# Softmax of the taps on one partition, exchanged weight halves by DMA, and the last product split

## The chip, the cores and the metric

The kernel runs on one core of a Trainium2 chip. A core has TensorE (PE; its weight loads are listed as PEld), VectorE (DVE), ScalarE (ACT), GpSimd (POOL) and SyncE (SP), which work from queues of their own and wait for each other by semaphores, and 16 DMA engines that all queues share. SP and ACT issue DMAs whose descriptors are made by hardware (queue q1 and q10 in the profile); POOL issues DMAs whose descriptors are made by software (q0). The metric is the time on the device of one execution in microseconds (us), less is better.

## The reference

Two stages in a row. First a light convolution along the sequence: x has 8 sequences of 3904 tokens of 192 channels, a softmax over 7 taps is made for each of 8 heads, and each head's 24 channels are summed over the current and the six tokens before with these taps. Then a multiplicative feed-forward over all 31232 tokens.

```python
w = softmax(weight)                       # 8 heads x 7 taps
out = np.einsum('hk,bskhg->bshg', w, x_unf)   # 7 tokens, ending at s
...
a = x @ w1                                # 192 -> 1024
b = x @ w2                                # 192 -> 1024
h = a * b @ w3                            # 1024 -> 1024
return (h @ w_out).astype(np.float32)     # 1024 -> 192
```

## The kernel before

The tokens are cut into two halves of 15616 (r = 0, 1) that are worked on side by side: partitions 0 to 63 belong to the one and 64 to 127 to the other, in x, in the convolution and in the transposed activations.

*Convolution.* x comes in blocks of windows of 64 tokens (58 new ones each; `SIZES`), loaded by POOL and cast to bf16 (`load_x`, and `load_first` for the very first window, lines 89 to 130). The taps are turned into band matrices `Aband`: the softmax (lines 178 to 191, on all 128 partitions, each having its own copy of the 8 x 7 taps by the DMA of line 133) gives `wsb`; `band_taps` (line 203) multiplies it with shifted diagonals into `cprod`; `band_sum` (line 210) adds these up on PE with an identity and with a swapped identity. `conv` multiplies a block's windows with the bands. Block 0 is convolved in lines 427 to 430 before all else; blocks 1 and 2 between rounds of the first two products.

*First product* (`first_product`, line 340). For each chunk R of 512 tokens of each half there are 8 rounds ft, one for each 128 of the 1024 columns. In a round PE makes pa = x w1 and pb = x w2 of both halves, 6 matmuls of 64 rows each, ACT copies pa to bf16, and DVE multiplies the copy by pb into `abT`. The work of `between` is put behind the round that it names: in chunk 0 the convolution of block 1 stands behind rounds 2 and 4 and its transposes behind round 6.

*Why halves are exchanged.* A matmul of half r reads x on partitions 64 r to 64 r + 63, and needs its 64 rows of the weights on the same partitions. `wn` holds the weights as loaded (three tiles), `wsw` the same with the two halves of the partitions exchanged; `w_of` chooses between them. `load_w` loads columns in two parts, 0 to 767 and 768 to 1023. `swap_w(k, part, engines)` copies one part of `wn[k]` to `wsw[k]` in two instructions; the parts are set by `WC`:

```python
WC = (0, DFF // 2, DFF * 3 // 4, DFF)
```

Part 0 of k = 0 and 2 and all of parts 1 and 2 are copied by POOL, part 0 of k = 1 by DVE and ACT.

*Second product* (`second_product`, line 367). w3 and w_out are multiplied together once (`W_sb`), so each chunk's `abT` is multiplied by `W_sb` alone: 8 matmuls for each 128 tokens, into one PSUM tile for a chunk and half. ACT copies the tile to SBUF and SP stores it. The last chunk has 256 tokens, so its last product has 16 matmuls, one copy of 384 columns, and one store.

*Warm-ups.* `warm(n)` gives PE n matmuls on zeros, whose results are not read: 18 at the start (line 172), two ahead of the first product (`lead=2`).

*Order.* The order of the instructions on each engine is that of the program text (`manual_schedule`); the framework adds the waits. POOL's queue holds, in this order: x of block 0, the first window, the masks (identity and diagonals), `load_w` of 768 columns, x of block 1, the four copies of part 0, `load_w` of the last 256 columns, x of block 2, the twelve copies of parts 1 and 2, w_out, w3, x of blocks 3 and 4. SP issues nothing before the stores of convolved rows of block 2. All PSUM tiles take turns in four buffers.

Of the kernel before, what the change touches and what calls it, by code (L numbers as in the profile page):

```python
# [8 lines left out]
FP32 = mybir.dt.float32  # L9
BF16 = mybir.dt.bfloat16  # L10
AX = mybir.AxisListType
ALU = mybir.AluOpType
# [4 lines left out]
def kernel(  # L17
# [10 lines left out]
    nc = tc.nc  # L28

    B, S, D = x.shape  # L30
    H, K = weight.shape
    G = D // H
    DFF = moe_w1.shape[1]
# [3 lines left out]
    NS = 2  # L37
# [28 lines left out]
    def banks(name):  # L66
        return psum.tile([128, NS, CH], FP32, tag="banks", name=name)
# [4 lines left out]
    def slot(shape, dtype, name):  # L72
        return stage.tile(shape, dtype, tag="slot", bufs=5, name=name)
# [15 lines left out]
    def load_x(b, parts=(0, 1)):  # L89
        tiles = xb_of.setdefault(b, [])  # L90
        zeros_of = zero_rows.setdefault(b, [])
        for i0, n in [v for e, v in enumerate(halves_of(b)) if e in parts]:
            xb = work.tile([128, n, D], BF16, tag="xb", bufs=6, name="xb")
            w = 0
            if i0 == 0:
                nc.vector.memset(xb[:, 0, :], 0.0)
                for r in range(NS):
                    nc.gpsimd.dma_start(out=xb[Q * r:Q * r + Q, 1:n, :], in_=x_spans(r, 1, n - 1))
                w = n
            while w < n:  # L100
                i = i0 + w
                m = min(n - w, WB - i % WB)
                at_end = i + m == NWIN
                if at_end:
                    m -= 1
                if m:
                    for r in range(NS):
                        nc.gpsimd.dma_start(out=xb[Q * r:Q * r + Q, w:w + m, :],  # L108
                                            in_=x_spans(r, i, m))
                if i % WB == 0:  # L110
                    zeros_of += [(xb, 0, w), (xb, 1, w)]
                w += m
                if at_end:
                    nc.gpsimd.memset(xb[Q:128, w, :], 0.0)
                    t = tok(NWIN - 1) - PAD
                    nc.gpsimd.dma_start(out=xb[0:Q, w, :], in_=x_rows[t:t + Q, :])
                    nc.gpsimd.dma_start(out=xb[Q:Q + PAD + LAST, w, :],
                                        in_=x_rows[TS + t:TS + t + PAD + LAST, :])
                    w += 1
            if len(halves_of(b)) == 1:  # L120
                tiles += [(xb, 0), (xb, SIZES[b] // 2)]
            else:
                tiles.append((xb, 0))


    def load_first():
        xb = xb_of[0][0][0]
        for r in range(NS):
            nc.gpsimd.dma_start(out=xb[Q * r + PAD:Q * r + Q, 0, :],
                                in_=x_rows[r * TS:r * TS + ST, :])  # L130

    wall = const.tile([128, H, K], FP32)
    nc.scalar.dma_start(out=wall, in_=weight.partition_broadcast(128))
    load_x(0)
    load_first()

    tiny = const.tile([128, 1], FP32)
    nc.vector.memset(tiny, 0.0)
# [2 lines left out]
    nc.scalar.activation(out=tiny, in_=tiny, func=ACT.Exp)  # L141

    ones = const.tile([128, 1], BF16)
    nc.gpsimd.memset(ones, 1.0)
    identw = const.tile([128, 128 + Q], BF16)
    diag = const.tile([128, Q + PAD], BF16)
    for m in (identw[:, 0:128], identw[:, 128:128 + Q], diag[0:Q], diag[Q:128]):
# [19 lines left out]
    def warm(n, t=None):  # L167
        t = banks("warm") if t is None else t
        for j in range(n):
            nc.tensor.matmul(t[:, j % 2, :], zeros[:, 0:128], zeros, start=True, stop=True)  # L170

    warm(18)


    wmax = const.tile([128, H], FP32)
    wsum = const.tile([128, H], FP32)
    wsb = const.tile([128, 2, 2, K], BF16)
    nc.vector.reduce_max(out=wmax, in_=wall, axis=AX.X)
    nc.vector.tensor_tensor(
        out=wall, in0=wall, in1=wmax.unsqueeze(2).to_broadcast([128, H, K]), op=ALU.subtract)  # L180
    nc.scalar.activation(out=wall, in_=wall, func=ACT.Exp)
    nc.vector.reduce_sum(out=wsum, in_=wall, axis=AX.X)
    nc.vector.reciprocal(out=wsum, in_=wsum)
    for r in range(NS):
        ps = slice(Q * r, Q * r + Q)
        nc.vector.tensor_tensor(
            out=wsb[ps],
            in0=wall[ps].rearrange("p (g a e) k -> p g a e k", g=2, a=2)[:, :, r],
            in1=wsum[ps].rearrange("p (g a e) -> p g a e", g=2, a=2)[:, :, r].unsqueeze(3)
                .to_broadcast([Q, 2, 2, K]),  # L190
            op=ALU.mult)

    Aband = const.tile([128, 2, 2, 2, Q], BF16)

# [142 lines left out]
    def width(R):  # L337
        return min(CH, TS - R * CH)

    def first_product(R, between=None, lead=0):  # L340
        N = width(R)
        ab = work.tile([128, JT, NS, CH], BF16, tag="abT", bufs=LAG + 1, name="abT")
        abT_of[R] = ab
        r0 = (R * CH) % RING
        for ft in range(JT):
            pq = []
            for i in range(2):
                p = banks("pa" if i == 0 else "pb")
                pq.append(p)
                if ft == 0 and i == 0:  # L350
                    warm(lead, p)
                for k in range(NP):
                    for r in range(NS):
                        rs = slice(Q * r, Q * r + Q)
                        nc.tensor.matmul(  # L355
                            p[:, r, 0:N], w_of(i, k, r)[rs, ft * 128:(ft + 1) * 128],
                            xT[k][rs, r0:r0 + N],
                            start=(k == 0), stop=(k == NP - 1))
            pa, pb = pq
            asb = work.tile([128, NS, CH], BF16, tag="asb", bufs=3, name="asb")  # L360
            nc.scalar.copy(out=asb[:, :, 0:N], in_=pa[:, :, 0:N])  # L361
            nc.vector.tensor_tensor(out=ab[:, ft, :, 0:N], in0=asb[:, :, 0:N],  # L362
                                    in1=pb[:, :, 0:N], op=ALU.mult)
            if between and ft in between:
                between[ft]()

    def second_product(R, r):
        ab = abT_of[R]
        ng = width(R) // 128
        ops = banks("ops")  # L370
        for g in range(ng):
            for jt in range(JT):
                nc.tensor.matmul(  # L373
                    ops[:, g // 2, (g % 2) * D:(g % 2) * D + D],
                    ab[:, jt, r, g * 128:(g + 1) * 128], W_sb[:, jt, :],
                    start=(jt == 0), stop=(jt == JT - 1))
        osb = slot([128, ng, D], FP32, "osb")
        nc.scalar.copy(out=osb.rearrange("p (a g) d -> p a (g d)", g=2),  # L378
                       in_=ops[:, 0:ng // 2, 0:2 * D])
        t0 = r * TS + R * CH  # L380
        nc.sync.dma_start(
            out=out[t0:t0 + ng * 128, :].rearrange("(g p) d -> p g d", p=128), in_=osb)
        if r == 1:
            del abT_of[R]

# [62 lines left out]
    def seq(*fs):  # L448
# [42 lines left out]
    for p, rounds in enumerate(phases):  # L491
        b, e = PROLOGUE_BLOCKS + p // 2, p % 2
        if b < NB:
            for xb, r, w in zero_rows.pop(b, []):
                nc.gpsimd.memset(xb[Q * r:Q * r + PAD, w, :], 0.0)
        for j, R in enumerate(rounds):
            first_product(R)
            if j == 0 and b + 1 < NB:
                P(out=pace, in_=abT_of[R][0:1, JT - 1, 1, 0:2])  # L499
                load_x(b + 1, (0, 1) if p == 1 else (e,))  # L500
        last = NR if p == len(phases) - 1 else done + 2
        for i in range(done, last):
# [39 lines left out]
```

## Time and profile before

| | us |
|---|---|
| median of 3 runs | 530.91 (530.59 to 531.13) |
| profiled execution, its own time | 530.57 |
| its span, first to last instruction | 528.9 |
| TensorE busy | 521.7 |
| first matmul of the first product | 12.55 |
| last matmul ends | 524.64 |

The profile page gives busy times of engines over the span, the chain of work that ended last (followed back from the last instruction to what released each step), groups of instructions by line, and the DMA queues. A row of a timeline is: start in us, length in us, engine, line, operation, output <- inputs, shapes, count, and in brackets how long the engine had been idle and what ended that. "PEclk" on the page is the clock that the throttle granted; it is at 9 tenths or more in all 40 slices.

### The profile page before, as it was taken

To read this page: it belongs to the slowest core of one execution; us is meant where nothing else is said; L and a number is where in the kernel's file an instruction comes from. 1 tells how busy PE (TensorE), PEld (TensorE's weight loads), DVE (VectorE), ACT (ScalarE), POOL (GpSimd) and SP (SyncE) were. 2 spreads that over 40 slices of the span, in tenths; PEclk is the share of its full clock that TensorE was granted. 3 is DMA by queue.
4 is the path that set the end of the run, shared out by engine and by line. 5 is a ranking of instruction groups with operands and counts; after the bars stand their busy time and mean duration, and the time that the engine had idled before them with its cause. 6 is when DMAs were issued, how large, how long until landed. Compare 5 with 4: busy or idle time off the path is not lost.

```text
span 528.9 us, 12698 instructions
## 1 busy us (share of the span) xinstructions
PE 521.7 (99%) x5469; PEld 351.0 (66%) x5469; DVE 359.3 (68%) x337; ACT 316.2 (60%) x348; POOL 54.8 (10%) x102
## 2 busy tenths in 40 slices
PE   8999999999999999999999999999999999999996
PEld 4555975857658576585765857667585574846676
DVE  4779459397593976949669496794957849386460
ACT  3887557375573755737467374664746647375652
POOL 8841002011010100201001010020000000000000
PEclk9999999999999999999999999999999999999999
DMA  9999559979562894636956379554725055240204
GB/s 117 110 206 191 116 96 189 184 165 143 131 90 95 173 132 131 87 114 138 147 148 70 123 147 135 133 56 134 150 81 120 1 151 127 78 90 23 99 2 151
DMA packets 130541, 63.13 MB, mean 119 GB/s; under 512 B 83352, under 2 KB 129460, under 8 KB 130484
## 3 DMA queue, kind: packets, MB, share of 16 engines
q1 hardware_dynamic: 91764, 45.65, 35.7%
q0 software_dynamic: 38576, 16.63, 27.0%
q8 instruction: 43, 0.70, 0.6%
q14 instruction: 14, 0.11, 0.1%
q10 hardware_dynamic: 144, 0.03, 0.0%
HBM read 33.28 MB, written 34.82 MB: 129 GB/s over the span
## 4 chain that ended last, share of the span: by engine, by line
PE 96%; DVE 2%; ACT 1%; issue 0%; ACTq 0%
PE ops L373 31%; PE pa L355 30%; PE pb L355 29%; PE cps L249 2%; PE warm L170 1%; DVE abT L362 1%; ACT asb L361 1%; PE wps L413 1%; PE tps L302 1%; PE w3ps L404 0%; PE bps L215 0%; ACT convo L266 0%; DVE w3T L407 0%; DVE convo L423 0%; ACT osb L378 0%
## 5 line engine op out<-in xcount | busy, mean ns | idle before, releaser
L362 DVE TENSOR_TENSOR abT<-asb,pb 128x1024 bf16<-128x1024 bf16 (+1 forms) x248 | 298.3, 1204 | 45.8 <-ACT asb L361 29.3
L361 ACT CAST asb<-pa 128x1024 bf16<-128x1024 f32 (+1 forms) x248 | 247.6, 998 | 70.4 <-PE pa L355 69.7
L355 PE MATMUL pb<-xT,wn 64*128 64x512 bf16 (+1 forms) x744 | 201.8, 372 | 0.2
L355 PE MATMUL pa<-xT,wn 64*128 64x512 bf16 (+1 forms) x744 | 197.9, 373 | 0.5
L355 PE MATMUL pa<-xT,ws 64*128 64x512 bf16 (+1 forms) x744 | 198.0, 373 | 0.0
L355 PE MATMUL pb<-xT,ws 64*128 64x512 bf16 (+1 forms) x744 | 193.8, 373 | 0.0
L355 PEld LDWEIGHTS <-wn 64*128 64x128 bf16 x1488 | 138.7, 94 | 79.8 <-issue 4.8
L355 PEld LDWEIGHTS <-ws 64*128 64x128 bf16 x1488 | 129.0, 94 | 68.4 <-issue 3.3
L373 PEld LDWEIGHTS <-abT 128*128 128x128 bf16 x1952 | 159.7, 98 | 9.7 <-issue 9.7
L373 PE MATMUL ops<-W_sb,abT 128*128 128x192 bf16 x1952 | 165.7, 246 | 0.0
L378 ACT COPY osb<-ops 128x768 f32<-128x768 f32 (+1 forms) x62 | 48.8, 788 | 127.1 <-PE ops L373 127.1
L266 DVE CAST convo<-cps 128x864 bf16<-128x864 f32 (+7 forms) x65 | 52.0, 847 | 98.4 <-PE cps L249 96.8
L108 POOL DMA_DIRECT2D xb<-in_x_dram x38 | 29.9, 799 | 13.0 <-DMA w3b<-in_moe_w_dram 5.1
L499 POOL COPY pace<-abT 1x2 bf16<-1x2 bf16 x9 | 1.6, 175 | 266.2 <-DVE abT L362 266.2
L249 PE MATMUL cps<-xb,Aband 64*64 64x432 bf16 (+3 forms) x320 | 17.8, 309 | 0.4 <-DVE abT L362 0.2
L249 PEld LDWEIGHTS <-Aband 64*64 64x64 bf16 x320 | 5.8, 105 | 6.7 <-issue 5.7
L170 PE MATMUL warm<-zeros 128*128 128x512 bf16 x18 | 6.9, 572 | 1.4 <-DVE zeros L140 1.4
L266 ACT CAST convo<-cps 128x640 bf16<-128x640 f32 (+4 forms) x13 | 7.4, 606 | 0.8 <-PE cps L249 0.8
L332 POOL COPY ws<-wn 64x256 bf16<-64x256 bf16 (+1 forms) x16 | 7.2, 449 | 0.9
L413 PE MATMUL wps<-wo_b,w3T 128*128 128x192 bf16 x64 | 6.3, 246 | 0.1
L170 PEld LDWEIGHTS <-zeros 128*128 128x128 bf16 x20 | 2.5, 134 | 5.4 <-issue 3.8
L413 PEld LDWEIGHTS <-w3T 128*128 128x128 bf16 x64 | 5.1, 98 | 1.0 <-issue 0.7
(51 smaller groups left out, 59.6 us busy)
## 6 DMA issues: line engine op xcount, KB each, us to landing
out_dram<-osb SPq DMA_DIRECT2D x60, 384.0 KB, 3.0
xb<-in_x_dram POOLq DMA_DIRECT2D x14, 432.0 KB, 8.0
rows<-convo SPq DMA_DIRECT2D x7, 648.0 KB, 9.3
xb<-in_x_dram POOLq DMA_DIRECT2D x8, 384.0 KB, 10.5
w3b<-in_moe_w_dram POOLq DMA_DIRECT2D x8, 256.0 KB, 8.7
rows<-convo SPq DMA_DIRECT2D x3, 576.0 KB, 5.4
xT<-rows SPq DMA_TRANSPOSE x84, 2.8
rows<-convo SPq DMA_DIRECT2D x2, 540.0 KB, 8.8
```

What stands on the lines that cost most here:

```text
L108: nc.gpsimd.dma_start(out=xb[Q * r:Q * r + Q, w:w + m, :], in_=x_spans(r, i, m))
L170: nc.tensor.matmul(t[:, j % 2, :], zeros[:, 0:128], zeros, start=True, stop=True)
L249: nc.tensor.matmul(view(slice(Q * c, Q * c + Q), r)[:, :, j * G:(j + 1) * G], band_of(h, r), xb[Q * r:Q * r + Q, w0:w0 + n, h * G:(h + 1) ...
L266: f[e % len(f)](out=dst, in_=part)
L302: nc.tensor.transpose(out=tps[:, w, :], in_=convo[:, w, k].rearrange("p r g -> p (r g)"), identity=ident)
L332: f(out=wsw[k][d:d + Q, cs], in_=wn[k][e:e + Q, cs])
L355: nc.tensor.matmul(p[:, r, 0:N], w_of(i, k, r)[rs, ft * 128:(ft + 1) * 128], xT[k][rs, r0:r0 + N], start=(k == 0), stop=(k == NP - 1))
L361: nc.scalar.copy(out=asb[:, :, 0:N], in_=pa[:, :, 0:N])
L362: nc.vector.tensor_tensor(out=ab[:, ft, :, 0:N], in0=asb[:, :, 0:N], in1=pb[:, :, 0:N], op=ALU.mult)
L373: nc.tensor.matmul(ops[:, g // 2, (g % 2) * D:(g % 2) * D + D], ab[:, jt, r, g * 128:(g + 1) * 128], W_sb[:, jt, :], start=(jt == 0), stop ...
L378: nc.scalar.copy(out=osb.rearrange("p (a g) d -> p a (g d)", g=2), in_=ops[:, 0:ng // 2, 0:2 * D])
L413: nc.tensor.matmul(wps[:, 0, 0:D], w3T[:, gt, :], wo_b[:, gt, :], start=(gt == 0), stop=(gt == JT - 1))
```

## The change

Four things change.

1. The weights of the taps are loaded to one partition; the softmax runs on it, `wrow` holds the result, and two matmuls with one row each spread it to the 128 partitions: `half` is a row of 64 zeros, 64 ones and 64 zeros, of which a window with the ones at the front or at the back is taken as the stationary operand, so that each half of the partitions gets the heads it needs. DVE copies the PSUM tile `wbc` to `wsb`. Warm-ups are 7 before and 4 behind these matmuls, where there were 18 in all, and the two ahead of the first product go.
2. `ones` is set by DVE and not by POOL, and POOL makes the two diagonal masks before `load_first` and the two parts of the identity after it.
3. Part 0 of the exchanged halves is now columns 0 to 255, part 1 is 256 to 767, part 2 is 768 to 1023. Part 0 is copied by the engines that did so before; parts 1 and 2 are copied by twelve DMAs that SP issues, in place of twelve copies on POOL. Rounds 0 and 1 read part 0, rounds 2 to 5 part 1, rounds 6 and 7 part 2.
4. The last product of the last chunk is made as two PSUM tiles of 128 tokens; DVE copies the first and SP stores it, ACT copies the second and issues its store itself.

```diff
-    wall = const.tile([128, H, K], FP32)
-    nc.scalar.dma_start(out=wall, in_=weight.partition_broadcast(128))
+    wall = const.tile([1, H, K], FP32)
+    nc.scalar.dma_start(out=wall, in_=weight.rearrange("(o h) k -> o h k", o=1))
     load_x(0)
-    load_first()
...
-    nc.gpsimd.memset(ones, 1.0)
+    nc.vector.memset(ones, 1.0)
+    half = const.tile([1, 3 * Q], BF16)
+    nc.vector.memset(half, 0.0)
+    nc.vector.memset(half[:, Q:2 * Q], 1.0)
...
+    diagonal(diag[0:Q])
+    diagonal(diag[Q:128])
+    load_first()
+    diagonal(identw[:, 0:128])
+    diagonal(identw[:, 128:128 + Q])
...
-    WC = (0, DFF // 2, DFF * 3 // 4, DFF)
+    WC = (0, DFF // 4, DFF * 3 // 4, DFF)
...
-    warm(18)
+    warm(7)
...
-    for r in range(NS):
-        ps = slice(Q * r, Q * r + Q)
-        nc.vector.tensor_tensor(
-            out=wsb[ps],
...
+    nc.vector.tensor_tensor(
+        out=wrow, in0=wall, in1=wsum.unsqueeze(2).to_broadcast([1, H, K]), op=ALU.mult)
+    wbc = banks("wbc")
+    wbc = wbc[:, 0, 0:H * K // 2].rearrange("p (g e k) -> p g e k", g=2, e=2)
+    wrow = wrow.rearrange("p (g a e) k -> p g a e k", g=2, a=2)
+    for a in range(2):
+        nc.tensor.matmul(wbc, half[:, Q - Q * a:Q - Q * a + 128], wrow[:, :, a],
+                         start=(a == 0), stop=(a == 1))
+    nc.vector.tensor_copy(out=wsb, in_=wbc)
+    warm(4)
...
-    def second_product(R, r):
+    def second_product(R, r, split=False):
...
+        parts = [(g, g + 1) for g in range(ng)] if split else [(0, ng)]
+        for e, (g0, g1) in enumerate(parts):
...
+            (nc.vector.tensor_copy if split and e == 0 else nc.scalar.copy)(
+                out=osb.rearrange("p (a g) d -> p a (g d)", g=n),
+                in_=ops[:, 0:m // n, 0:n * D])
+            t = t0 + g0 * 128
+            (nc.scalar if split and g1 == ng else nc.sync).dma_start(
+                out=out[t:t + m * 128, :].rearrange("(g p) d -> p g d", p=128), in_=osb)
...
+    S_DMA = nc.sync.dma_start
     load_x(1)
...
     swap_w(1, 0, (V, A))
+    for part in (1, 2):
+        for k in (0, 2, 1):
+            swap_w(k, part, (S_DMA, S_DMA))
     load_x(2)
-    for k in (0, 2, 1):
-        swap_w(k, 1, (P, P))
-    for k in (0, 2, 1):
-        swap_w(k, 2, (P, P))
...
-    first_product(0, lead=2, between={
+    first_product(0, {
...
-            second_product(i, 1)
+            second_product(i, 1, i == NR - 1)
```

More of the change, by code (lines that the diff above doesn't have):

```diff
@@ L143, with diagonal @@
     ones = const.tile([128, 1], BF16)
-    nc.gpsimd.memset(ones, 1.0)
+    nc.vector.memset(ones, 1.0)
+    half = const.tile([1, 3 * Q], BF16)
+    nc.vector.memset(half, 0.0)
+    nc.vector.memset(half[:, Q:2 * Q], 1.0)
     identw = const.tile([128, 128 + Q], BF16)
     diag = const.tile([128, Q + PAD], BF16)
-    for m in (identw[:, 0:128], identw[:, 128:128 + Q], diag[0:Q], diag[Q:128]):
+    def diagonal(m):
         p, n = m.shape
@@ L170, in warm @@
             nc.tensor.matmul(t[:, j % 2, :], zeros[:, 0:128], zeros, start=True, stop=True)
-    warm(18)
-    wmax = const.tile([128, H], FP32)
-    wsum = const.tile([128, H], FP32)
+    warm(7)
+    wmax = const.tile([1, H], FP32)
+    wsum = const.tile([1, H], FP32)
+    wrow = const.tile([1, H, K], BF16)
     wsb = const.tile([128, 2, 2, K], BF16)
@@ L179 @@
     nc.vector.tensor_tensor(
-        out=wall, in0=wall, in1=wmax.unsqueeze(2).to_broadcast([128, H, K]), op=ALU.subtract)
+        out=wall, in0=wall, in1=wmax.unsqueeze(2).to_broadcast([1, H, K]), op=ALU.subtract)
     nc.scalar.activation(out=wall, in_=wall, func=ACT.Exp)
@@ L183 @@
     nc.vector.reciprocal(out=wsum, in_=wsum)
-    for r in range(NS):
-        ps = slice(Q * r, Q * r + Q)
-        nc.vector.tensor_tensor(
-            out=wsb[ps],
[L188 to L191, printed above, removed]
+    nc.vector.tensor_tensor(
[8 more added lines that the diff above has]
+    warm(4)
     Aband = const.tile([128, 2, 2, 2, Q], BF16)
@@ L338, in width, with first_product @@
         return min(CH, TS - R * CH)
-    def first_product(R, between=None, lead=0):
+    def first_product(R, between=None):
         N = width(R)
@@ L349, in first_product @@
                 pq.append(p)
-                if ft == 0 and i == 0:
-                    warm(lead, p)
                 for k in range(NP):
@@ L365, in first_product @@
                 between[ft]()
-    def second_product(R, r):
+    def second_product(R, r, split=False):
         ab = abT_of[R]
         ng = width(R) // 128
[L370 to L379, printed above, removed]
-        t0 = r * TS + R * CH
-        nc.sync.dma_start(
-            out=out[t0:t0 + ng * 128, :].rearrange("(g p) d -> p g d", p=128), in_=osb)
+        t0 = r * TS + R * CH
+        parts = [(g, g + 1) for g in range(ng)] if split else [(0, ng)]
+        for e, (g0, g1) in enumerate(parts):
+            m = g1 - g0
+            ops = banks("ops")
+            for g in range(m):
+                for jt in range(JT):
+                    nc.tensor.matmul(
+                        ops[:, g // 2, (g % 2) * D:(g % 2) * D + D],
+                        ab[:, jt, r, (g0 + g) * 128:(g0 + g + 1) * 128], W_sb[:, jt, :],
+                        start=(jt == 0), stop=(jt == JT - 1))
+            osb = slot([128, m, D], FP32, "osb")
+            n = min(m, 2)
+            (nc.vector.tensor_copy if split and e == 0 else nc.scalar.copy)(
[4 more added lines that the diff above has]
+                out=out[t:t + m * 128, :].rearrange("(g p) d -> p g d", p=128), in_=osb)
         if r == 1:
```

## The prediction

> **What bounds the kernel now.** I read the engines' shares first, then the whole chain, then the chain's first 17 us, the timeline of each engine there, the landings of the early transfers, and last the closing microseconds.
>
> Shares of busy time and the chain, from the page:
>
> ```profile
> PE 521.7 (99%) x5469; PEld 351.0 (66%) x5469; DVE 359.3 (68%) x337; ACT 316.2 (60%) x348; POOL 54.8 (10%) x102
> ...
> PE 96%; DVE 2%; ACT 1%; issue 0%; ACTq 0%
> ```
>
> TensorE is the chain almost from end to end, so a microsecond saved on DVE, ACT or POOL in the middle is worth nothing. What is left is the head, until the first product runs, and the tail after the last matmul. The chain's head (start, length, what):
>
> ```profile
> 1.39 6.95 PE warm L170 x18
> 8.33 1.58 PE bps L215 x28
> ...
> 11.07 1.12 PE tps L302 x15
> ...
> 12.62 0.76 PE pa L355 x6
> ```
>
> The 18 warm-up matmuls themselves are the chain until 8.33, the band sums then take 56 ns a matmul. The same stretch in the timelines of the engines:
>
> ```profile
> 0.82 0.38 ACTq L133 DMA_DIRECT2D wall<-in_weight_dram  x1
> 4.71 0.21 DVE L178 TENSOR_REDUCE wmax<-wall 128x8 f32<-128x56 f32 x1 [3.37 <-DMA wall<-in_weight_dram]
> 5.97 0.38 DVE L186 TENSOR_TENSOR wsb<-wall,wsum 64x28 bf16<-64x28 f32 x2
> 6.46 2.09 DVE L205 TENSOR_TENSOR cprod<-diag,wsb 128x896 bf16<-128x896 bf16 x2
> 6.48 0.15 PEld L170 LDWEIGHTS <-zeros 128*128 128x128 bf16 x1 [0.28 <-issue]
> 6.91 0.15 PEld L170 LDWEIGHTS <-zeros 128*128 128x128 bf16 x1 [0.28 <-issue]
> 9.05 2.59 POOL L332 COPY ws<-wn 64x512 bf16<-64x512 bf16 x4
> 16.62 0.41 PE L249 MATMUL cps<-xb,Aband 64*64 64x120 bf16 x16
> ```
>
> The taps arrive 3.9 us after their issue and hold DVE idle for 3.37. The warm-ups come 0.43 us apart until 6.91, half the rate of the later matmuls. The last row is the convolution of block 1, between the rounds of the first product. What it reads, x of block 1, was issued in two transfers (those issued between 8.15 and 8.9, and the one running then):
>
> ```profile
> L108 POOL DMA_DIRECT2D xb<-in_x_dram x2: 799/802/804, 7.4 to 8.1; - x2
> ...
> DMA to landing us min/median/max: 6.5/6.8/7.0
> ```
>
> So it lands at 13.9 and 15.15, 1.5 us before PE asks. What an SP transfer meets while POOL's queue is full: SP issued two stores of `rows` at 31.58 and 32.01. The queues in 31.5 to 35.1 and then in 35.1 to 37:
>
> ```profile
> q0 software_dynamic: 426, 0.74, 111.6%
> ```
> ```profile
> q0 software_dynamic: 593, 0.24, 100.8%
> q1 hardware_dynamic: 258, 0.18, 39.1%
> ```
>
> The first answer has no q1 at all: for 3.5 us the SP queue moved no packet. In 11.2 to 15.2 the engines are as full (DMA share 1.28). At the end:
>
> ```profile
> 524.71 0.48 ACT osb L378
> ```
> ```profile
> SPq L537 <- DMA out_dram<-osb: 1.4, 3, 0.5
> ```
>
> After the last copy (525.19) only the last store and the closing waits remain until 528.86.
>
> **The change, part by part.** The sum stands against the profiled execution: 530.57 us, of which 528.9 are span.
>
> *Softmax on one partition.* 128 rows of 224 bytes become one. The last store of the kernel is issued at 525.21; SP's closing waits on the stores (1.4 us from 525.6, and their instructions) put its landing at 527.2, 2.0 us on an idle queue; the quickest median on the page is 2.8. Bounds for the taps: 2.7 to 3.6; I take 2.75, being so much smaller than a 192 KB store. DVE's first maximum to the first product took 5.97 - 4.71 = 1.26, its lengths hardly depend on the number of partitions, so the product runs at 4.0 to 4.2 (one instruction of 0.18 is saved). New on the path: two matmuls of one row, and a DVE copy out of PSUM. Seven warm-ups of 0.43 end at 4.4, so PE is free just then; the two with their weight loads (0.13 each) and a small matmul's 0.21 end at 4.85. The copy has no row: 0.18 (same width from SBUF) to 0.29 (the 160-wide cast), taken 0.2. The band products start at 5.1 and not at 6.46, and end at 6.15 and 7.2. Four warm-ups fill PE to 6.3; nine band matmuls at half rate until 7.3, five and then 14 at 56 ns, end at 8.35 against 9.91: **1.5 us earlier** (0.7 if the taps need until 3.6). Nothing behind it changes length: casts, the convolution of block 0, transposes. The two lead warm-ups (0.43 on the chain) free at most 0.1, since the copies of xT end at 12.58 and 12.69, right where they end. Hidden: three small DVE memsets (0.06 each) under the wait for the taps; POOL's diag masks, 0.58, go ahead of the first window's two loads, which then land at about 8.0 at the latest (3.52 + 3.9 + 0.58), convolution 0 asks at 8.3. Were that cover gone, it would cost under 0.6.
>
> *Exchanged halves.* POOL's first four copies shrink from 512 to 256 columns (0.61 to 0.40 each): 9.05 to 10.9, wn[2]'s landing at 10.06 included; needed at 11.4. ACT's and DVE's copies of k=1 halve too. POOL loses twelve copies (5.31 us, 15.29 to 20.6), so w_out and w3 are issued from about 14 to 16 on and not 20.55; nobody asks for them before 48, worth nothing. Added: twelve SP issues of 0.37 (SP has nothing else before 31.58), each waiting for a wn load: 9.0 (k=0), 10.06 (k=2), 11.2 (k=1). Every first-product matmul from the third round on now reads what these bring. Rounds take 1.3, so with 1.5 gained the third asks for k=0 and 2 at 13.7, for k=1 at 14.3. Six transfers of 64 KB, last issued at 11.6. Idle 2.0: landed 13.6. By the 31.58 row (3.5 until the first packet, about 1.7 to move): 16.8. By amount: the 0.18 MB of q1 took 39% of 1.9 us, so 0.39 MB take 1.6 us of engine time, at a share of 1.28 some 1.2. I take 15.0 (2.0, 1.2, and 0.2 of waiting); of the two ends this is nearer the idle one, since at 9 to 12 far less is queued ahead of them than w3's eight loads at 31.
>
> The Trainium skill, "DMA: Bandwidth & Descriptors", section "Queues, rings and completion order", says that an engine takes turns between its queue rows packet by packet. By that the halves would never wait long and the sum would keep my 15.0; the 31.58 row does not look like turns, and by it the sum would be the second rival's.
>
> *What is late next.* x of block 1: PE now asks at 16.62 - 1.5 = 15.1 and it lands at 15.15 even undisturbed. The halves travel among its packets: 0 to 1.6 later, taken 1.0. So the convolution starts at 16.15, after 0.7 already lost on k=1: **head 1.5 - 1.05 = 0.45 us**. Part 2's halves follow the last wn landings (15.5 to 16.3), land by 18.5 to 21 and are asked for at about 21: nothing, with little cover.
>
> *Tail.* PE does the same 16 matmuls. The last ACT copy is 192 wide: 0.80 for 768 and 0.48 for 384 give 0.32, saving 0.16; no hop to SP; 96 KB instead of 192 at the tail's 237 to 260 GB/s: 0.4 less, of which the other half's store, ending beside it, takes some; SP's closing waits may be fewer behind the last landing, 0 to 0.3. Bounds 0.2 to 0.8, **taken 0.6**.
>
> Sum: 530.57 - 0.45 - 0.6 = 529.5. The profiled execution is the quickest of the four times shown; their mean is 530.8, so I say **529.7**.
>
> **Rivals.**
> *All arrives in time.* The halves take their turns, x of block 1 is hardly delayed: 530.8 - 1.5 - 0.6 = 528.7. For it: 128 reads fewer and POOL unburdened. Against: zero slack at 15.1.
> *The halves wait behind POOL's queue (slower side).* PE stands in the third round's second product until 16.8, 2.5 us, in place of everything gained: 530.8 - 1.5 + 2.5 - 0.6 = 531.2. For it: the 31.58 row. Against: that row stood behind eight loads of w3, these stand behind one of wn and one of x. It decides from a landing of 16.4 on, where head and tail are eaten; over 17.5 the kernel is slower by over 0.2%.
> *PE's rate stays at half.* With fewer warm-ups the half-rate stretch (1.39 to 6.91 here) may last 3 us longer: 28 band matmuls at 0.107 instead of partly 0.056 cost 1.0, the first convolution 0.4; then x of block 1 is no longer late: 530.8 - 0.1 - 0.6 = 530.1; were the first product's start caught too, up to 532. For it: the rate rose only after 5.5 us without a pause. Against: seven and four leave almost no pause. The Trainium skill, "TensorE: Matmul & The Clock Gate", Part 1, has full rate only after a busy window of about 3.4 us, free-running. The trace agrees in kind, its stretch was 5.5.
>
> **How the numbers follow.** Forecast 0.45, in time 0.20, halves late 0.18, half rate 0.14, other 0.03. A change under 0.2% (1.06 us) can't be told from none here; the bounds are 529.85 and 531.97. The forecast lies at the edge: 0.27 of its 0.45 is faster, 0.18 within. With all of the first rival: faster 0.47. Of the late halves 0.12 and of half rate 0.06 go over the upper bound, 0.03 other: slower 0.21. Same 0.32. Range 528.6 to 531.6; the forecast's own, with x 0.5 to 1.5 late and the tail's bounds, 529.0 to 530.4.
>
> **What would show it.** The maximum on DVE starts at 2.7 to 3.6; band products at 5.1; the band matmuls end near 8.35 with warm-ups still 0.43 apart; the first product starts at 11; PE's gap of about 1 us before the convolution of block 1, released by a transfer of xb, or earlier in the third round, by the exchanged halves; the last copy 0.3 long. I am wrong if that gap is missing or over 2 us, or if band matmuls are still 0.107 apart after 8.

## The result and the profile after

The changed kernel takes 534.80 us (median of 6 runs, 534.03 to 536.95), the kernel before 530.85 in the same comparison: a ratio of the means of 1.0083, 95% interval 1.0062 to 1.0103. It is **slower by 0.8%**, where 529.7 and a gain were forecast, with a range of 528.6 to 531.6. The profiled execution took 534.39, with a span of 532.7. Two executions far off all others, one of 904 us of the exchanged halves by DMA alone and one of 1392 us of the kernel before, are left out of the figures below.

The shares of busy time and of the chain, from the page of the changed kernel:

```profile
PE 522.7 (98%) x5462; PEld 348.0 (65%) x5462; DVE 359.9 (68%) x341; ACT 315.9 (59%) x348; POOL 49.3 (9%) x89
...
PE 94%; DMA 2%; DVE 1%; ACT 1%; POOL 1%; issue 0%; SPq 0%; POOLq 0%; ACTq 0%
```

TensorE works only one microsecond longer than before (522.7 against 521.7); the chain, though, has 2% of DMA in it, where it had none. These are the two pieces shown below, 6.45 and 5.44 us, more than the loss itself, since DMA has taken the place of the warm-ups and of some of the work there. The timeline of the head, with the same columns as before:

```profile
2.04 0.20 DVE L188 TENSOR_REDUCE wmax<-wall 1x8 f32<-1x56 f32 x1 [0.42 <-DMA wall<-in_weight_dram]
5.05 2.10 DVE L217 TENSOR_TENSOR cprod<-diag,wsb 128x896 bf16<-128x896 bf16 x2
6.21 1.96 PE L227 MATMUL bps<-cprod,identw 128*128 128x128 bf16 x28
9.07 11.85 SPq L344 DMA_DIRECT2D ws<-wn  x12
10.39 0.39 PE L365 MATMUL pa<-xT,wn 64*128 64x512 bf16 x1
13.29 0.39 PE L365 MATMUL pb<-xT,wn 64*128 64x512 bf16 x1 [1.36 <-DMA wn<-in_moe_w_dram]
16.22 0.39 PE L365 MATMUL pa<-xT,ws 64*128 64x512 bf16 x2 [0.38 <-DMA ws<-wn]
19.25 0.51 PE L365 MATMUL pb<-xT,ws 64*128 64x512 bf16 x2 [1.87 <-DMA ws<-wn]
20.54 0.61 PE L261 MATMUL cps<-xb,Aband 64*64 64x120 bf16 x16
```

The softmax does what it was meant to: the taps are there at 2.04 and not 4.71, the band sums end at 8.17 and not 9.9, and the first product starts at 10.39 and not 12.55, 2.2 us earlier. Then PE stands three times for longer than 0.3 us, once for wn[1] and twice for the exchanged halves of part 1, and reaches the convolution of block 1 at 20.54, where it was at 16.62: from 2.2 us ahead to 3.9 behind within 10 us. The chain of waits there (start, length, what):

```profile
6.79 6.45 DMA wn<-in_moe_w_dram
13.24 0.02 issue
13.26 0.46 SPq L344
13.72 0.04 issue
13.76 5.44 DMA ws<-wn
19.21 0.04 issue
19.25 1.35 PE pb L365 x5
```

The load of wn[1] takes 6.45 us, then SP sends its exchanged halves, and the second of them, 64 KB, takes 5.44 us. Three windows in the order of time (length, busy time of PE, its weight loads, DVE, ACT and POOL with the numbers of instructions, granted clock, share of the DMA engines, GB/s):

```profile
12.57:15.99 3.42, 2.50 (x19) 0.89 (x19) 1.44 (x2) 2.18 (x3) 3.42 (x5) 1.00 1.42 225
15.99:19.40 3.41, 1.14 (x8) 0.32 (x10) 1.22 (x1) 1.26 (x2) 2.44 (x5) 1.00 1.52 197
19.40:22.81 3.41, 3.41 (x31) 1.15 (x29) 1.22 (x1) 1.24 (x3) 1.33 (x3) 0.50 1.39 200
```

After a window with PE busy for a third, the clock is granted at half for the next 3.41 us. The rest of round 2, the convolution and most of round 3 run at half rate there, and the distance to before grows from 3.9 us at the convolution to 5.0 at the transposes of block 1 (28.02 against 23.02). From there on nothing changes any more: the last matmul ends 5.0 us later (529.66 against 524.62 by the rows of the timelines). The tail gives back 1.2: from the last matmul's end to the end of the span 3.02 us, where it was 4.24. The fall of the clock is not needed for the loss: one fall of 3.41 us lowers the mean granted clock of an execution by 0.003, and of the six executions of the changed kernel the one with a mean of 1.000 took 534.03, the five with 0.993 to 0.997 took 534.38 to 536.95.

### The profile page after: what moved, and what is told of

Same layout as the page of the kernel before. It is cut to its first block, busy times and chain, and to the rows that moved or that the text cites. A ratio compares the mean times of both kernels' runs of the same rounds, so it can differ in the third digit from the quotient of the medians.

```text
span 532.7 us, 12696 instructions
## 1 busy us (share of the span) xinstructions
PE 522.7 (98%) x5462; PEld 348.0 (65%) x5462; DVE 359.9 (68%) x341; ACT 315.9 (59%) x348; POOL 49.3 (9%) x89
## 4 chain that ended last, share of the span: by engine, by line
PE 94%; DMA 2%; DVE 1%; ACT 1%; POOL 1%; issue 0%; SPq 0%; POOLq 0%; ACTq 0%
PE ops L387 31%; PE pa L365 29%; PE pb L365 29%; PE cps L261 3%; DMA wn<-in_moe_w_dram 1%; PE wps L429 1%; DMA ws<-wn 1%; DVE abT L372 1%; ACT asb L371 1%; PE w3ps L420 0%; POOL xb L98 0%; PE tps L314 0%; POOL xb L129 0%; ACT xT L326 0%; DVE w3T L423 0%
## 5 line engine op out<-in xcount | busy, mean ns | idle before, releaser
L393 ACT COPY osb<-ops 128x768 f32<-128x768 f32 (+2 forms) x62 | 48.8, 787 | 127.0 <-PE ops L387 127.0
L179 PE MATMUL warm<-zeros 128*128 128x512 bf16 x11 | 4.7, 595 | 1.4 <-DVE ones L143 1.4
L414 POOL DMA_DIRECT2D w3b<-in_moe_w_dram x8 | 4.3, 544 | 3.6 <-DMA wo_b<-in_moe_w_out_dram 1.8
```

What stands on the lines that cost most here:

```text
L393: (nc.vector.tensor_copy if split and e == 0 else nc.scalar.copy)(out=osb.rearrange("p (a g) d -> p a (g d)", g=n), in_=ops[:, 0:m // n, 0 ...
L414: nc.gpsimd.dma_start(out=w3b_of[jt], in_=w3r[:, jt, :])
```

## The experiments

All times below are medians; the ratios are of the means to the kernel before, timed beside each run, with their 95% intervals. Starts of marked instructions are from the one profiled execution of each; landings of single transfers are from the trace's semaphore records.

### The head alone

The kernel before with the softmax, the order of the masks and the warm-ups of the change; `swap_w`, `WC` and the last product as before. The edit is shown against the changed kernel.

```diff
-    WC = (0, DFF // 4, DFF * 3 // 4, DFF)
+    WC = (0, DFF // 2, DFF * 3 // 4, DFF)
...
-    for part in (1, 2):
-        for k in (0, 2, 1):
-            swap_w(k, part, (S_DMA, S_DMA))
     load_x(2)
+    for k in (0, 2, 1):
+        swap_w(k, 1, (P, P))
+    for k in (0, 2, 1):
+        swap_w(k, 2, (P, P))
...
-            second_product(i, 1, i == NR - 1)
+            second_product(i, 1)
```

> The kernel before with the softmax on one partition, the order of the masks and the fewer warm-ups alone; exchanged halves by engine copies and the last product in one tile, as before. Theory (the halves by DMA are the loss: they hold up the load of wn[1] and land late themselves, the clock falls in the gap): without them the head is a gain. Bands end at about 8.2, the first product starts at about 10.4, waits for POOL's copy of k=2 until 11.65 in place of 12.8, wn[1] lands at 11.2 as before; 0.8 to 1.0 us less than before, 529.9, clock at full rate from about 7 on. Rival (the early start is the loss: fewer warm-ups let the clock fall, or PE comes before its weights): slower than before, 532 to 534, with half rate somewhere before 23 us.

530.34 us, ratio 1.0003 (0.9994 to 1.0013): no change, so both expectations missed. The profiled execution (533.49) is the slowest of eleven, which begin at 529.59, and shows one way in which the gain can go. Two windows of it, with the columns of the windows above:

```profile
10.47:13.89 3.42, 2.46 (x18) 0.75 (x17) 0.80 (x3) 1.73 (x3) 3.30 (x7) 1.00 1.28 157
13.89:17.30 3.41, 3.41 (x20) 1.23 (x18) 1.37 (x2) 1.54 (x2) 3.23 (x7) 0.50 0.92 94
```

With no SP transfer at all, wn[1] landed at 12.74 (15 of its 16 engines were done at 11.15), PE waited 0.33 us each for POOL's copies and for wn[1] and 0.26 for ACT's copy, and the clock fell for 3.41 us. So the early start does make PE outrun its weights, and the clock can fall by it: that much of the rival is true in this execution. The other ten have a mean granted clock of 0.998 to 1.000, so no fall, and still their median is that of the kernel before. Where the gain of the head went in them is not shown.

### The split of the last product alone

```diff
-            second_product(i, 1)
+            second_product(i, 1, i == NR - 1)
```

(with the changed `second_product` in the kernel before.)

> The kernel before with the last product in two PSUM tiles alone. From the last matmul's end to the end of the span the kernel before takes 4.2 us and the changed one 3.0. Theory: the split alone gives that, 1.2 us less, 529.6. Rival (the order of the queue's lanes at the closing waits gives most of it, and the twelve added transfers shift it): 0.3 to 0.6 us less, 530.4.

530.26 us, ratio 0.9994 (0.9985 to 1.0003), within the noise; the tail is 3.88 us against 4.24. So the split gives 0.36 of the tail's 1.2, as the rival had it. The two ends, first the kernel before, then this one:

```profile
524.71 0.48 ACT L378 COPY osb<-ops 128x384 f32<-128x384 f32 x1 [0.89 <-PE ops L373]
```
```profile
524.40 0.32 ACT L383 COPY osb<-ops 128x192 f32<-128x192 f32 x1 [0.89 <-PE ops L377]
```

The copy is 0.16 shorter. The last store landed 2.26 us after the last matmul and not 2.56.

### The exchanged halves by DMA alone

```diff
-    WC = (0, DFF // 2, DFF * 3 // 4, DFF)
+    WC = (0, DFF // 4, DFF * 3 // 4, DFF)
...
+    for part in (1, 2):
+        for k in (0, 2, 1):
+            swap_w(k, part, (S_DMA, S_DMA))
     load_x(2)
-    for k in (0, 2, 1):
-        swap_w(k, 1, (P, P))
-    for k in (0, 2, 1):
-        swap_w(k, 2, (P, P))
```

> The kernel before with the exchanged halves by DMA alone (parts of 256, 512 and 256 columns, twelve SP transfers, order k = 0, 2, 1). Theory: wn[1] lands at about 13.2 and not 11.2, the halves of k=1 at about 19 against a request at 16.0, so PE stands for about 3 us in round 2, and the clock falls: 534 to 536. Rival (they only hurt because the head became earlier): PE asks 2 us later, so under 1 us of standing and no fall of the clock: 531 to 532.

534.86 us (three executions), ratio 1.0091 (1.0072 to 1.0110): this part alone makes the whole loss, and the rival falls. The time lies in the 534 to 536 that I had expected, but by luck, since it comes about in another way. PE's longest waits between 9 and 30 us (in all, times, longest):

```profile
PE pa L355 <- DMA ws<-wn: 1.9, 3, 1.1
PE pb L355 <- DMA ws<-wn: 1.7, 2, 1.2
```

Here the clock never fell, and round 2 cost only part of it: PE was at the convolution of block 1 at 18.19, 1.6 behind. The largest waits came later, in round 6:

```profile
25.61 0.39 PE L355 MATMUL pa<-xT,ws 64*128 64x512 bf16 x1 [1.06 <-DMA ws<-wn]
27.27 0.39 PE L355 MATMUL pb<-xT,ws 64*128 64x512 bf16 x2 [1.19 <-DMA ws<-wn]
```

The halves of part 2 landed from 23.1 to 27.2. The transposes of block 1 start at 28.02, in the changed kernel at 28.02 too. Two rows of the changed kernel, round 6's second product and the transposes:

```profile
27.27 0.39 PE L365 MATMUL pb<-xT,ws 64*128 64x512 bf16 x2
28.02 1.01 PE L314 MATMUL tps<-identw,convo 128*128 128x128 bf16 x15
```

In both, the last half of part 2, landed at 27.23, leaves no earlier time, and what happened before it in round 2 is hidden behind it. The changed kernel came to that point within 0.2 us of the landing, by way of its waits in round 2 and the half rate; there the two limits fall together.

### All but the halves by DMA

The changed kernel, with the engine copies of before:

```diff
-    WC = (0, DFF // 4, DFF * 3 // 4, DFF)
+    WC = (0, DFF // 2, DFF * 3 // 4, DFF)
...
-    for part in (1, 2):
-        for k in (0, 2, 1):
-            swap_w(k, part, (S_DMA, S_DMA))
     load_x(2)
+    for k in (0, 2, 1):
+        swap_w(k, 1, (P, P))
+    for k in (0, 2, 1):
+        swap_w(k, 2, (P, P))
```

> The changed kernel with the exchanged halves by engine copies as before, all else changed. Theory: the head's 0.9 and the tail's 1.2 add up, 528.7, faster than both. Rival (early start is the loss): 531 to 533.

529.48 us, ratio 0.9986 (0.9973 to 0.9999), just faster: the rival is out, and the theory's 528.7 is not reached. The last matmul ends at 523.50, 1.1 before the kernel before, the tail is 3.74. In this execution wn[1] landed at 11.19 and the convolution of block 1 ran at 15.23, against 18.46 in the run of the head alone, whose code for the head is the same.

### Transfers that nobody reads

The last kernel, plus the twelve transfers of the change into tiles of their own.

```diff
+    spare = [const.tile([128, DFF], BF16, name=f"sp{k}", tag=f"sp{k}") for k in range(3)]
+    for c0_, c1_ in ((DFF // 4, DFF * 3 // 4), (DFF * 3 // 4, DFF)):
+        for k in (0, 2, 1):
+            for d, e in ((0, Q), (Q, 0)):
+                S_DMA(out=spare[k][d:d + Q, c0_:c1_], in_=wn[k][e:e + Q, c0_:c1_])
     load_x(2)
     for k in (0, 2, 1):
         swap_w(k, 1, (P, P))
```

> The changed kernel with engine copies of the halves (as in the run without DMA swaps, 529.5), plus the same twelve SP transfers into tiles that nobody reads. It parts what the transfers do to others from what waiting for them costs. Theory (most of the loss is waiting for late halves, a smaller part is what they take from wn[1] and x of block 1): wn[1] lands at 12 to 13 and not 11.2, x of block 1 at about 16, PE loses 1 to 1.5 us by it, the lanes of the closing waits give back 0.7: 529.5 to 530.5. Rival (the transfers mainly hold up POOL's loads): wn[1] and x as in the changed kernel and 533 or more.

529.62 us, ratio 0.9993 (0.9973 to 1.0012). The last matmul ends at 524.86, 1.4 later than without the transfers, and 4.8 earlier than in the changed kernel. So of the 6.2 us by which the halves by DMA put off the last matmul (529.66 against 523.50), about 1.4 is what the transfers do to others, and 4.8 is waiting for them and what follows from it. This parting is of one execution each, and those of this run lie between 528.09 and 533.47; by the medians and the tails the first share is 0.85. POOL still copies the halves here, so w_out is issued at 21.51, and the twelve transfers had all landed by 22.46; what POOL does when it is freed of these copies belongs to the 4.8. wn[1] landed at 12.82 and x of block 1 at 15.92. These landings and the time are as the theory had them.

### w_out and w3 held back

```diff
+    spare = const.tile([Q, DFF // 4], BF16)
+    for k in (0, 2, 1, 0, 2, 1):
+        for e in (0, Q):
+            P(out=spare, in_=wn[k][e:e + Q, DFF // 2:DFF * 3 // 4])
     load_wo()
```

> The changed kernel, with twelve idle copies of 256 columns on POOL ahead of w_out, so that w_out and w3 are issued at about 20 as before and not from 15. Theory (SP transfers crawl while POOL's queue is full, and freeing POOL filled it): part 2's halves take 2 to 4 us and not 5.8 to 6.9, all landed by 23 and not 27.2. PE gains little by it, 0.3 to 0.5 us, since it comes to round 6 only at about 26 after the standing in round 2 and the half rate behind it: 534.3. Rival (SP's own order and issue time set their landing): still 5.8 us or more each, landed at 27, time as the changed kernel's, 534.8.

533.41 us, ratio 1.0052 (1.0032 to 1.0072), 1.4 less than the changed kernel. w_out was issued at 19.75 (15.05 in the changed kernel), and part 2's halves took 3.8, 3.5, 2.9, 2.5, 2.0 and 1.8 us, all landed by 21.20; in the changed kernel the same six took 5.8 to 6.9, the last landed at 27.23. The queues between 17 and 23 us (q0 is POOL's, q1 SP's; packets, MB, share of the engines), first of the changed kernel, then of this one:

```profile
q0 software_dynamic: 2248, 1.09, 137.3%
q1 hardware_dynamic: 195, 0.10, 7.9%
```
```profile
q0 software_dynamic: 1103, 0.41, 65.0%
q1 hardware_dynamic: 480, 0.20, 12.9%
```

With POOL's queue full SP's transfers moved 195 packets in these 6 us; with it all but empty from 18.5 to 21 us (71 packets of POOL's, 374 of SP's), all 480. So POOL's later loads are what makes part 2 late, and the rival, SP's own order and issue time, is out. The theory was right on the landings; on the time it was short, since it gave 0.3 to 0.5 us and 1.4 came. Part 1, sent while POOL's queue was as full as ever, still took 5.5 to 6.1 each. No run sends part 1 into an empty queue, so for part 1 the same cause is argued and not tested.

In the profiled execution the clock was at half from 16.3 to 23.1. The eight executions show what that costs: the two with a mean granted clock of 1.000 took 530.92 and 531.54 us, the six with 0.993 to 0.997 took 532.70 to 535.31. With part 2 out of the way the half rate is thus a loss of its own, while in the changed kernel the one execution without a fall was only 0.35 us ahead of the next.

### PE's gap filled

```diff
-    def first_product(R, between=None):
+    def first_product(R, between=None, fill=0):
...
                 pq.append(p)
+                if ft == 2 and i == 1:
+                    warm(fill, p)
...
-    first_product(0, {
+    first_product(0, fill=9, between={
```

> The changed kernel with nine matmuls on zeros ahead of the second product of round 2, where PE stands for 1.9 us. Theory (the last of part 2's halves, landing at 27.2, is what sets the end of the first chunk): the clock stays at full rate, PE reaches round 6 some 1.1 us sooner and then waits for part 2: no change, 534.4 to 535. Rival (the half rate is a loss of its own): 1 to 1.7 us less, 533.4.

536.52 us, ratio 1.0116 (1.0101 to 1.0131): 1.7 more than the changed kernel, which neither expected. The clock did stay up through round 2, though the nine matmuls run from 17.70 to 19.82 and the last half of part 1 had landed at 18.39, so they hold PE longer than the wait would have. PE was at the second half of the convolution of block 1 at 23.52, 1.1 sooner than in the changed kernel. But then it waited for part 2. PE's waits between 9 and 30 us:

```profile
PE pa L367 <- DMA ws<-wn: 2.7, 3, 1.1
PE pb L367 <- DMA ws<-wn: 1.2, 1, 1.2
```

The last half of part 2 landed at 28.61 in this execution, 1.4 later than in the changed kernel, and the wait for it brought the clock down after all:

```profile
26.20:29.60 3.40, 1.51 (x12) 0.58 (x12) 1.14 (x2) 1.01 (x1) 2.10 (x3) 1.00 1.13 212
29.60:33.00 3.40, 3.40 (x25) 1.87 (x24) 1.57 (x2) 1.82 (x3) 2.07 (x3) 0.50 1.19 203
```

So the sooner arrival is lost at part 2, as the theory had it; that the run became slower is put down to the later landing, of which I can't say why, and to the fall of the clock behind it. All four executions have a mean granted clock of 0.996 or 0.997, so it fell in each.

### Both

```diff
+                if ft == 2 and i == 1:
+                    warm(fill, p)
...
+    spare = const.tile([Q, DFF // 4], BF16)
+    for k in (0, 2, 1, 0, 2, 1):
+        for e in (0, Q):
+            P(out=spare, in_=wn[k][e:e + Q, DFF // 2:DFF * 3 // 4])
     load_wo()
...
-    first_product(0, {
+    first_product(0, fill=9, between={
```

> Both edits of the last two at once: idle copies on POOL and filled gap. Theory (two limits behind one another, part 2's landing and the half rate): only together do they give 1.2 to 1.8 us, 533.2. Rival (either is worth its own part alone): the sum of the two single runs, whatever they are.

532.88 us, ratio 1.0048 (1.0033 to 1.0063), 1.9 less than the changed kernel. Alone, the filled gap cost 1.7 and the held loads gave 1.4, so the rival's sum is 535.1 and is out. But "only together" is not shown either: the ratio is that of the held loads alone (1.0048 and 1.0052, with intervals that overlap). With part 2 out of the way the filled gap no longer costs anything; that it helps can't be told from these times. What it does is keep the clock up: all four executions have a mean of 0.999 to 1.000 and lie between 532.83 and 533.56, where those of the held loads alone spread from 530.92 to 535.31. In the profiled execution the transposes of block 1 start at 25.97 (27.12 with the held loads alone, 28.02 in the changed kernel). What is left of the loss is round 2's waits of 1.3 and 0.9 us for part 1, and the nine matmuls themselves, which end at 18.89 though the last half of part 1 had landed at 17.43.

### k = 1 first

```diff
     for part in (1, 2):
-        for k in (0, 2, 1):
+        for k in (1, 0, 2):
             swap_w(k, part, (S_DMA, S_DMA))
```

> The changed kernel with the order k = 1, 0, 2 of SP's transfers in both parts, so that SP sends nothing before wn[1] has landed. Theory (each transfer takes what POOL's backlog makes it take, 4.5 to 6.5 us here): nothing disturbs wn[1], which lands at 11.0 to 11.4; the six of part 1 are issued from then to 14.5 and land at 16.5 to 20; PE then stands for k = 0 and 2 in round 2, as long as it did for k = 1, and part 2 lands at 26 to 28: 534 to 536, no better. Rival (the order is the fault, k = 1 standing last behind wn[1]): 1 us or more less than the changed kernel.

538.40 us, ratio 1.0147 (1.0133 to 1.0161): the rival is out, and the theory's 534 to 536 was too low. wn[1] landed at 12.57, although SP had sent nothing before it, so here it was not early SP transfers that put it off. All twelve went out behind it, and k = 0, now second, was late by more than k = 1 had been:

```profile
20.21 0.54 PE L365 MATMUL pa<-xT,ws 64*128 64x512 bf16 x2 [5.04 <-DMA ws<-wn]
```

With five microseconds of standing the clock was at half for two stretches, from 20.33 to 27.16.

### The lanes of the closing waits

The kernel with all but the DMA halves, and four SP transfers of 128 bytes that nobody reads. A lane is one of the eight semaphores that SP's and ACT's transfers take in turn, and by which their landing is told.

```diff
     warm(7)
+
+    pad = const.tile([1, 4, Q], BF16)
+    for j in range(4):
+        nc.sync.dma_start(out=pad[:, j, :], in_=zeros[0:1, 0:Q])
```

> The kernel without DMA swaps (softmax, masks, warm-ups and split as changed) with four SP transfers of 128 bytes ahead, which nobody reads and which only shift by four the lanes that the stores use. Theory (the tail was 3.0 us in the changed kernel and in the spare run, 3.7 without the twelve transfers, because the last store then falls on the lane that SP's closing waits ask for last): the tail is 3.0 us and the time 528.8. Rival (the tail differs by something else): tail 3.7, time 529.5.

528.94 us, ratio 0.9970 (0.9958 to 0.9981): faster than the kernel before and the changed one, clear of the noise. Against the kernel without the four transfers (0.9986, 0.9973 to 0.9999) the time alone would not show a gain for certain; the trace does, the tail is 3.07 us as expected, where it was 3.74. From the landing of the last store to the end of the span are 1.6 to 1.7 us in the kernel before, in the split alone and in the kernel without these transfers, and 0.9 to 1.0 with them, in the changed kernel, in the halves alone, and in the two runs with the filled gap. The last store's semaphore is the third of eight lanes before, the fourth with the split, and the last with four or twelve transfers more on top (the seventh in the halves alone, where the end is as quick); SP asks for the lanes one after another at the end. That their order makes the difference fits all these runs; the waits themselves were not taken apart.

The four transfers show one thing more. Sent at 1.36, 2.04, 2.65 and 3.28 us, while POOL's first loads of x came up, they landed after 1.7, 3.5, 4.1 and 3.6 us, with 128 bytes each: under POOL's loads a transfer on SP's queue is late even where there is next to nothing to move.

### POOL's order

```diff
-    load_x(2)
     for k in (0, 2, 1):
         swap_w(k, 1, (P, P))
+    load_x(2)
...
-    first_product(0, {
+    first_product(0, lead=2, between={
```

(and `lead` as in the kernel before.)

> The same with part 1 of POOL's copies ahead of the loads of x of block 2, and two warm-ups ahead of the first product again, where PE waits for POOL's first copies until 11.67. Theory: the wait of 0.4 us on POOL's copies at 18.0 goes, the warm-ups lie in the wait and keep the clock up in more of the runs: 528.4, the median 0.3 to 0.5 us under the run with the lanes alone. Rival (they lie on the path, or x of block 2 comes late): 0.2 to 0.5 us more than it.

529.11 us, ratio 0.9972 (0.9961 to 0.9984): the same as the last within the noise; neither expectation. In the profiled executions PE still waits 0.72 and 0.77 us at the start of the first product for POOL's first copies, which wait for wn[2] (landed at 10.8 and 11.0), and that may be what swallows the gain that the order was to bring.

## Why the prediction was wrong

*Softmax on one partition.* Right in mechanism, and better than forecast. The taps were there at 2.04, below my lower bound of 2.7: a store of 192 KB was no bound from below for a read of 224 bytes, which took 1.2 us from its issue. The early taps gained nothing, though: the softmax was done at 3.70 and PE busy with the seven warm-ups until the two matmuls at 4.49, so that the band products started at 5.05 (said 5.1) is the warm-ups' doing. The band sums ended at 8.17 (8.35). I gave the two lead warm-ups 0.1 us; they gave 0.4 (from the end of the band sums to the first product 2.22 us, before 2.64). With all of it, the first product started 2.2 us earlier and not 1.6.

*When the halves land: the step that failed.* I had two ends, 13.6 on an idle queue and 16.8 by the stores that SP had sent into POOL's full queue at 31.58, and took 15.0, "nearer the idle one, since far less is queued ahead". The last half of part 1 landed at 19.2 in the changed kernel, at 21.6 with k = 1 first, and at 17.4 to 18.4 in the runs of the halves alone, with the gap filled, with w_out held, and with both. So the sum's head term, 0.45 us gained, came out as the last matmul 5.0 us later. The row that I had set aside was the right one: the twelve transfers took 4.7 to 6.9 us each, as the first of the stores had (5.5, landed at 37.11), though a different load was queued in front. The first packet of SP's queue moved at 13.28, 4.2 us after the first issue. No run sends part 1 while POOL's queue is empty, so this cause is shown for part 2 and argued for part 1. Nothing of "less is queued ahead" showed: x of block 1, the last columns of the weights, x of block 2, w_out and w3 followed each other without a break. When the queue was empty, with w_out held, the last two of part 2 took 2.0 and 1.8, my idle price. The rival of the halves waiting behind POOL's queue was thus the right one in kind, and its rule held in the changed kernel, that from a landing over 17.5 on the kernel is slower by over 0.2%; it had 0.18, and 531.2 at its price, because it knew round 2 alone.

By the Trainium skill, "DMA: Bandwidth & Descriptors", section "Queues, rings and completion order", an engine takes turns between its queues' packets. The trace of the changed kernel agrees in one stretch: from 22 to 26 us SP's queue moved 388 packets and POOL's 412. It does not in another: from 18.4 to 21 us, with two to six of part 2's transfers sent and not landed, they moved 5 and 1288. There the measurement decides; why SP's packets did not come in between is open.

*Part 2: "nothing, with little cover".* The second failed step, and the larger one. I let part 2 land by 18.5 to 21, at the price of part 1, and counted w_out's and w3's earlier issue as "worth nothing", since nobody asks for them before 48. They were worth a loss: POOL, freed of 5.3 us of copies, filled its own queue earlier, and SP's transfers were late while it was full. Part 2 landed at 23.0 to 27.2, and in the run of the halves alone it held PE longer than part 1 did (2.6 us in round 6, 0.9 in round 2). Holding w_out and w3 back brought it to 21.2.

*wn[1].* I left its landing at 11.2. In the changed kernel it was 13.24, which cost PE its first wait and put off the sending of its halves. That early SP transfers cause this is not shown: it landed at 11.0 and 11.1 in two runs with them, and at 12.7 and 12.6 in two without any before it. What makes it vary between 11.0 and 13.2 I did not settle.

*x of block 1.* Landed 1.4 us later than before, at 16.56, as said (16.15), but nobody waited: PE came only at 20.5. A wait that I made the forecast's centre was hidden behind a longer one. The gap came in the third round instead, behind the exchanged halves, and with 0.38 and 1.87 us it is over the 2 us from which I had called myself wrong.

*The clock.* I looked for the half rate in the band sums, by the fewer warm-ups. There the clock came up at 5.7 us (7.3 before), nothing was lost. That says little of the warm-ups: over the thirteen profiled executions it came up anywhere between 4.5 and 7.3, and these two ends, the split alone and the kernel before, have the same code in the head. It fell where PE stood for its weights, and each fall lasted 3.41 us or twice that, in five profiled executions, and began a whole number of times 3.41 after the clock had come up (in the changed kernel four times, from 5.75 to 19.40). This is the free-running window of about 3.4 us of the Trainium skill, "TensorE: Matmul & The Clock Gate", Part 1; the trace agrees (3.41). My rival had the rule and not the place: it looked at the work removed and not at the waits added.

*Tail.* 0.6 taken, 0.8 the upper bound, 1.2 measured. The copy's 0.16 was right, and the store's share was 0.3; the closing waits gave 0.77 where I had allowed 0 to 0.3, and that not by the split but by the number of transfers sent since the start.

## What to carry to other kernels

In these runs a short transfer on SP's queue cost two microseconds only where POOL's queue was empty, and 4.7 to 6.9 in the changed kernel, where it was full; before putting copies of a busy engine on it, look at what the transfers that were sent into a full queue took, and take that, however different they look. Relieving a queue's engine brings its later loads forward, into the stretch in which the new transfers run, so what the freed engine does next belongs into the sum. And where PE comes to stand for more than half of a 3.4 us window, the wait may be paid for twice, by the wait and by half rate after it.

## What I had not expected of the hardware

- A DMA of 224 bytes into one partition was there 1.2 us after its issue, where the same weights to 128 partitions took 3.9. POOL's first packet moved at 2.95, after it had landed; 128 bytes on SP's queue, sent at 2.65 us under POOL's first loads, took 4.1.
- Counted in windows of 3.41 us from where the clock came up, it fell to half after windows in which PE was busy for 0.12, 1.14, 1.42 and 1.51 us, and it stayed up after 1.66 (k = 1 first), 1.96 and 2.06 (the halves alone) and 2.05 us (the transfers that nobody reads). One execution does not fit: in the head alone it fell after 2.46. It came back after windows in which PE was busy throughout, and stayed at half after 2.95 and 2.85 (k = 1 first, w_out held).
- The end of the span moves by 0.7 us with the number of DMAs that a kernel has sent, through the lane that the last one falls on: four idle transfers of 128 bytes were worth that.
